# Clustered attention with a softplus network: another issue order, other engines for the movable operations, and no split of V where nothing reads it

## The chip, the cores and the metric

The kernel runs on one core of a Trainium2 chip. The metric is device time in microseconds for one execution, as the median of several runs. A core has five engines with an instruction queue each: TensorE (PE; matmuls and transposes, results in PSUM), Vector (DVE), Scalar (ACT), Pool (GpSimd) and Sync (SP), which here issues the DMAs. Each queue runs in the order in which its instructions were written; engines wait for each other through semaphores.

## The reference

Four batches, eight heads, 768 positions, head dimension 64. Every query and every key is assigned to the nearest of 16 centroids of its head (by cosine), and a query attends only to keys of its own cluster. The result, 3072 rows of 512, goes through a two-layer network with softplus. Everything is float32.

```
q_assign = argmax(q_n @ c_n^T)      # per head; k_assign in the same way
mask     = q_assign[:, None] == k_assign[None, :]
scores   = where(mask, (q @ k^T) / sqrt(64), -1e9)
attn     = softmax(scores);  x = attn @ v          # x: 3072 x 512
h        = x @ w_in                                # 512 -> 2048
out      = (max(h, 0) + log1p(exp(-abs(h)))) @ w_out   # 2048 -> 512
```

## The kernel before

Float32 values are split in two float16 parts, high (a cast) and low (the value less its high part), and a product is the sum of three float16 matmuls (four with the mask). So nearly every operand needs a cast (line 276, `cast`) and a subtraction.

The work is cut into eight passes (batch, half of the positions) of eight heads with three query tiles each: 192 tiles, numbered t. Tile t belongs to head n, pass pi.

Preparation. `prep_k(n)` loads K of a pair of heads, casts it, subtracts, turns it (on TensorE for the first two pairs, by DMA for the others) into `kT0`, multiplies it with the centroids (`sim_k`, L562), marks the nearest one, counts the keys of each cluster (L701), and turns the marked form into `kT1`. A DMA (`lift`, L538) writes one extra row. `prep_q` and, for the first four heads of the first pass, `first_q` (in two halves u of two heads) do the same for q: products (`sim_q`), marks, the minimum with the live clusters (L868), the maximum of it (L869), the multiply of q's high part by it (L879) with a small one (L886), and the turn into `qT1`. `prep_v(n)` loads V of a pair, casts it into the middle columns of `vb` (`vh`) and subtracts into the first ones (`v`, L467). `prep_weights(step)` decodes one block of the weights (Scalar L390, Vector L392 and L396, a cast, a subtraction).

Tiles. The first 36 tiles (`UPRIGHT`) go the way of `upright(t)`: a masked product m (L942), its negated row maximum on Vector (L954), a transpose of that on TensorE (`turned`, L961), a copy `u` of it into the extra row of q, the product u (L981, L982) with keys on the partitions, and the exponential on Scalar (L1025), which gives float32 weights. Their value product (`attend`, L1137) uses the float32 V tile and float32 weights. The others go through `scores(t)`: product (L1051), row maximum (L1067), exponential (L1075), cast `ph`, subtraction `p` (L1089), for each pair of tiles one DMA transpose (`pt<-phl`, L295), and a value product of 18 float16 matmuls (L1141 to L1143) with both parts of V. `ffn1` and `softplus` follow for each pass (names `gh`, `g`), then `ffn2`; the last two passes use a form with seven products instead of eight.

Order. Each of these functions is a chain (a Python generator) that yields its operations one after the other. Nothing is planned at build time: `PLAN` is a string of base-36 numbers, two characters each, and entry by entry says which chain gives its next operation. So each engine's queue is the sequence of the operations of that engine in `PLAN`. `either(key, ...)` yields an operation that two engines can do; a name in `SWAPPED` takes the second one. A name is a kind and a tile, head, step or pass: `p41` is the subtraction of tile 41, `wh7` the cast of weight step 7. `FILL` gives, for TensorE's n-th operation, how many warm-up matmuls (L257: 128x120, results never read) are put ahead of it.

Buffers are rings: a chain that takes a buffer waits in TensorE's, Vector's or another queue until the old one is free.

Of the kernel before, what the change touches and what calls it, by code (L numbers as in the profile page):

```python
# [36 lines left out]
SWAPPED = ('E1_0', 'S1l_1', 'S1l_3', 'S2_1', 'S2_3', 'S2h_0', 'S2l_0', 'S3l_0', 'S3l_2', 'S4_0', 'S4_2', 'S4_3', 'S4h_2', 'S4l_1', 'S4l_2', 'T1a_0', 'T1a_2', 'T1c_0', 'T1c_3', 'T1h_3', 'T1l_1', 'T2a_2', 'T2c_1', 'T3a_0', 'T3a_1', 'T3a_2', 'T3a_3', 'T3b_0', 'T3b_1', 'T3b_2', 'T3c_1', 'T3l_1', 'T3l_3', 'T4c_0', 'T4h_2', 'T4h_3', 'T4l_0', 'T4l_2', 'g0_3', 'g0_5', 'g1_1', 'g2_5', 'g5_7', 'g6_0', 'g6_1', 'g6_4', 'g6_5', 'g6_6', 'g7_1', 'g7_2', 'g7_4', 'g7_5', 'g7_6', 'g7_7', 'gh1_6', 'gh2_4', 'gh3_1', 'gh5_6', 'gh7_0', 'gh7_2', 'gh7_3', 'gh7_5', 'k0_0', 'k0_1', 'k14', 'k18', 'k22', 'kT0_0_0', 'kT0_2_1', 'kT1_2_0', 'kT1_2_1', 'm12_2_0', 'm12_3_0', 'm20_4_0', 'm28_7_0', 'm8_2_0', 'm8_3_0', 'p100', 'p101', 'p103', 'p136', 'p170', 'p172', 'p173', 'p175', 'p177', 'p178', 'p180', 'p181', 'p182', 'p183', 'p184', 'p185', 'p186', 'p189', 'p190', 'p191', 'p38', 'p39', 'p40', 'p42', 'p45', 'p46', 'p47', 'p59', 'p61', 'p64', 'p67', 'p71', 'p72', 'p79', 'p82', 'p85', 'p89', 'p90', 'p92', 'ph175', 'ph178', 'ph180', 'ph184', 'ph186', 'ph189', 'ph58', 'ph62', 'ph83', 'ph86', 'ph87', 'q0_0_0', 'qT1_1', 'u1', 'u11', 'u13', 'u21', 'u23', 'u27', 'u31', 'u33', 'u35', 'v8', 'vh14', 'vh18', 'w15', 'w19', 'w20', 'w23', 'w29', 'wh17', 'wh24', 'wh29', 'wh30', 'wh7', 'wh9', 'x0_2', 'x2_0', 'x6_3', 'x7_0', 'x7_1', 'x7_2', 'x7_3', 'xh0_3', 'xh1_3', 'xh2_3', 'xh3_0', 'xh3_3', 'xh6_3', 'xh7_0', 'zk10', 'zk12', 'zk16', 'zk18', 'zk2', 'zk20', 'zk4', 'zq0_1', 'zq8_2')  # L37
# [10 lines left out]
    "1xc7c6c61zc61xc8c7c7c6c721211w23231z0a21211z1y210d252023ce0bcfc9cac8cbcc21caca25252723c822c9c9c8ca2723c92325"
    "2927270d2b22220a222925cdce25242b2b29272d29260d0dcccbcccecd2d2729292fcf222b28cc0ace2f2h2f0d2d2f2d2bcb22cccgch"
    "ci2h2j2a0d0d0dcgcg2b2h2dcf0dcf0d0dcd2j2c2d2f2e0dcf0dcf0d0d22cjcd2fcbcb2h2e2e2e2l2j2j0d0d2l2n2nchci2echcgch2g"  # L50
    "2h2h2j2l2n2lcgcgck2jch2nce2p2p2i2l2k2p2l2r2ncicicjci2p2rcdchcl2ncjcj2m2p2t2r0eckckckck2t2p2rcj2e2ecicmcjce2o"
    "2r2r2v2v2t2q2t2v2t2q2q2qcl2x0e0e0e2v2tck2q2q2s2v2v2x2z2z2x2xcmclcmclcm2ucn2q312z2x312w0e0e0e0e0e0eco2z2x2zcl"
    "2z33333131cl2y310fcncn0e0e0ecncz33353531cmcmcpcq33czcncococo33dpcn35cz37370f0f0fcoczdqdqdp353037320ecocr3335"
    "37dp0e0e0e39cz0hdqdqdq3232323439czcp32cqcpcpcqcq32323539370f0f3b3936dsdsdsczcpcp37crcq3b390fcrcrcrcr393d0fcz"
    "3bcz3b0ecs3d3d3b0f0f0f3dczdtdt0h3bdudu0f0fdtdt0hcqdt383d0i3d3f3f3aczctcscsducs3f3h3f3f3c3jcz3edv3h3jcscs0gcu"
    "0i0i0i3h3ld0ctdw3hct3h3hdw3edw3j0g3ncz3edv3edwczd0ctcu3l3n0i3j3l3pdy3edyctdwd0cu0g0j0kcucu3l3n3ndy3e3eczczdz"
    "3gdz0i3p0i3i3rcuctcv3l0iczcz3j3l3p3t3p0g3ndzczdz0iczdz3rd03p3pcve0e03t3r3ve0cz3ke10jcvcv3tcz3xe1cv3te23m0id0"
# [1634 lines left out]
```

## Time and profile before

| | |
|---|---|
| time, median of three runs (lowest to highest) | 811.96 us (811.94 to 812.08) |
| span of the profiled execution | 809.7 us |
| outside of the span (median less span) | 2.3 us |
| TensorE busy | 799.3 us, 99% |
| Vector, Scalar, Pool busy | 597.8, 548.4, 473.8 us |

The profile shows one execution. The span goes from the first to the last instruction; its own time is not given, and the difference to the median is taken to be the same before and after. A busy TensorE is not TensorE at its peak, since matmuls are pipelined and each is shown some 0.16 us longer than the distance to the next. Idle time of an engine counts only where the work that ends last waits for it.

### The profile page before, as it was taken

How to read it: one execution, taken by the hardware profiler on the slowest of the kernel's cores; microseconds unless marked ns; L12 is line 12 of the kernel's file. 1: busy time of each engine (PE TensorE's matmuls, PEld its weight loads, DVE VectorE, ACT ScalarE, POOL GpSimd, SP SyncE). 2: the span in 40 equal slices, each digit the busy share in tenths (PEclk: the TensorE clock that was granted, in tenths of full speed). 3: DMA queues.
4: the chain of work that ended last, by engine and by line, in shares of the span. 5: the costliest groups of instructions: out<-in, count | busy, mean ns of one | idle time of the engine just before them, and what ended most of it. 6: DMA issues, size and time to landing. Idle time of an engine off the chain costs nothing.

```text
span 809.7 us, 19600 instructions
## 1 busy us (share of the span) xinstructions
PE 799.3 (99%) x8086; PEld 543.1 (67%) x8086; DVE 597.8 (74%) x1005; ACT 548.4 (68%) x851; POOL 473.8 (59%) x351
## 2 busy tenths in 40 slices
PE   8999999999999999999999999999999999999998
PEld 8898987655666666656666656666666656576787
DVE  7889998887976877766664547658554868887796
ACT  6777689865877777658587577677676667645441
POOL 4645456555656577745677585687578562613453
PEclk9999999999999999999999999999999999999999
DMA  9976769999999999999899989999898687730101
GB/s 257 244 185 157 218 148 225 205 219 201 173 175 181 184 207 200 216 204 174 155 162 188 189 171 186 206 209 168 171 165 177 115 145 129 128 60 1 47 1 60
DMA packets 390474, 133.71 MB, mean 165 GB/s; under 512 B 367088, under 2 KB 383984, under 8 KB 390384
## 3 DMA queue, kind: packets, MB, share of 16 engines
q1 hardware_dynamic: 390384, 132.46, 81.8%
q8 instruction: 63, 1.03, 0.5%
q14 instruction: 27, 0.22, 0.1%
HBM read 35.68 MB, written 6.29 MB: 52 GB/s over the span
## 4 chain that ended last, share of the span: by engine, by line
PE 77%; DMA 5%; DVE 2%; ACT 1%; POOL 1%; issue 0%; SPq 0%; DVEq 0%; ACTq 0%; POOLq 0%
PE s L1051 11%; PE h L1212 9%; PE h L1214 9%; PE h L1213 9%; PE o L1613 7%; PE o L1615 7%; PE o L1614 7%; DMA pt<-phl 4%; PE mbank L1141 3%; PE mbank L1143 3%; PE mbank L1142 3%; PE m L1491 2%; PE m L1492 2%; PE m L1490 2%; PE mbank L1137 1%; POOL phl L1089 1%
## 5 line engine op out<-in xcount | busy, mean ns | idle before, releaser
L1089 POOL TENSOR_TENSOR phl<-p,phl 128x768 f16<-128x768 f32 x117 | 194.1, 1667 | 123.9 <-ACT phl L276 94.5
L1067 DVE TENSOR_REDUCE negm<-s 128x1 f32<-128x768 f32 x156 | 147.9, 952 | 51.1 <-PE s L1051 49.6
L1075 ACT ACTIVATE p<-s,negm 128x768 f32<-128x768 f32 x156 | 139.5, 896 | 65.9 <-DVE negm L1067 50.8
L1212 PE MATMUL h<-xT,wi 128*128 128x384 f16 x512 | 166.8, 326 | 0.4 <-DVE fg L1249 0.4
L1214 PE MATMUL h<-xT,wi 128*128 128x384 f16 x512 | 167.0, 326 | 0.0
L1213 PE MATMUL h<-xT,wi 128*128 128x384 f16 x512 | 166.9, 326 | 0.0
L276 ACT CAST phl<-p 128x768 f16<-128x768 f32 x145 | 118.7, 829 | 21.1 <-DMA pt<-phl 19.0
L1051 PE MATMUL s<-kt,qt 128*128 128x384 f16 x624 | 126.2, 326 | 0.0
L1233 ACT ACTIVATE fa<-h 128x384 f32<-128x384 f32 x128 | 62.3, 488 | 75.8 <-PE h L1214 75.2
L1613 PE MATMUL o<-wo,gh 128*128 128x512 f16 x288 | 109.1, 379 | 0.4 <-DVE ot L1636 0.4
L1615 PE MATMUL o<-wo,gh 128*128 128x512 f16 x288 | 109.2, 379 | 0.0
L1614 PE MATMUL o<-wo,gh 128*128 128x512 f16 x288 | 109.2, 379 | 0.0
L1249 DVE SCALAR_TENSOR_TENSOR fg<-fa,h 128x384 f32<-128x384 f32 x104 | 56.8, 549 | 62.3 <-ACT fa L1234 54.8
L1141 PE MATMUL mbank<-vb,pt 128*128 128x65 f16 x936 | 99.8, 193 | 0.8 <-DMA pt<-phl 0.7
L1142 PE MATMUL mbank<-vb,pt 128*128 128x64 f16 x936 | 99.8, 192 | 0.0
L1143 PE MATMUL mbank<-vb,pt 128*128 128x65 f16 x936 | 99.6, 194 | 0.0
L1141 PEld LDWEIGHTS <-pt 128*128 128x128 f16 x936 | 86.8, 98 | 12.6 <-DMA pt<-phl 2.4
L1142 PEld LDWEIGHTS <-pt 128*128 128x128 f16 x936 | 86.2, 97 | 10.0
L1272 POOL TENSOR_TENSOR gh<-fg,gh 128x768 f16<-128x768 f32 x43 | 72.3, 1683 | 27.7 <-ACT gh L276 27.5
L1143 PEld LDWEIGHTS <-pt 128*128 128x128 f16 x936 | 86.3, 97 | 0.0
L1051 PEld LDWEIGHTS <-qt 128*128 128x128 f16 x624 | 58.3, 98 | 39.8
L1214 PEld LDWEIGHTS <-wi 128*128 128x128 f16 x512 | 49.9, 98 | 33.2
(300 smaller groups left out, 1622.7 us busy)
## 6 DMA issues: line engine op xcount, KB each, us to landing
wo<-in_moe_w_in_dram SPq DMA_DIRECT2D x16, 512.0 KB, 5.1
wo<-in_moe_w_out_dram SPq DMA_DIRECT2D x14, 512.0 KB, 4.2
rawk<-in_k_dram SPq DMA_DIRECT2D x15, 384.0 KB, 4.4
rawq<-in_q_dram SPq DMA_DIRECT2D x15, 384.0 KB, 4.4
rawv<-in_v_dram SPq DMA_DIRECT2D x12, 384.0 KB, 4.1
out_dram<-ot SPq DMA_DIRECT2D x18, 256.0 KB, 2.7
rawv<-in_v_dram SPq DMA_DIRECT2D x8, 192.0 KB, 5.4
pt<-phl SPq DMA_TRANSPOSE x78, 5.9
```

The costliest lines, as they stand in the source:

```text
L1051: nc.tensor.matmul(st[:, j, :SH], qt[:, s, i], kt[:, s, NT // 2 * j : NT // 2 * (j + 1)], start=(s == 0), stop=(s == 1),)
L1067: yield op("DVE", 950, lambda: nc.vector.tensor_reduce(negm, st[:, :, :SH], AX.XY, ALU.max, negate=True))
L1089: lambda e: e.tensor_tensor(phl[:, u, 1], p32, phl[:, u, 0], ALU.subtract),
L1141: nc.tensor.matmul(av, pt[:, 0, c], vb[:, c, D : 2 * D + 1], start=(c == 0), stop=False)
L1142: nc.tensor.matmul(av[:, :D], pt[:, 0, c], vb[:, c, :D], start=False, stop=False)
L1143: nc.tensor.matmul(av, pt[:, 1, c], vb[:, c, D : 2 * D + 1], start=False, stop=(c == NT - 1))
L1212: nc.tensor.matmul(hp, w[0], x[0], start=(c == 0), stop=False)
L1213: nc.tensor.matmul(hp, w[0], x[1], start=False, stop=False)
L1214: nc.tensor.matmul(hp, w[1], x[0], start=False, stop=(c == NP - 1))
L1613: nc.tensor.matmul(po, g[0], wo[:, f, 0, 0], start=(f == f0), stop=False)
L1614: nc.tensor.matmul(po, g[0], wo[:, f, 0, 1], start=False, stop=False)
L1615: nc.tensor.matmul(po, g[1], wo[:, f, 0, 0], start=False, stop=(f == f0 + NF // 2 - 1))
```

## The change

Four things change, and no operation of the computation is different.

- `FILL` is a new table: 88 warm-up matmuls instead of 175.
- `SWAPPED` is a new list. 227 operations change sides: 86 go from Scalar to Pool and 11 from Pool to Scalar (all casts), 74 from Pool to Vector and 29 from Vector to Pool (subtractions and a few products), 17 from Vector to Scalar and 10 from Scalar to Vector (copies and marks).
- `PLAN` is a new string. TensorE's first operation and its last 398 of 1002 stand where they stood (the last third of the run), those between are in another order. The other queues' last 86 to 355 operations also stay.
- `prep_v` leaves out the cast and the subtraction for the pairs of heads of which no tile needs split V: pairs 0 and 1 of the first batch. Two casts (`vh0`, `vh2`) and two subtractions (`v0`, `v2`) go. A small operation also gets a name of its own (`mw_0`, `mw_1`; it was `m0_0_0`, `m0_0_1` like the one ahead of it), so that it can have its own side.

```
-FILL = {0: 40, 3: 12, 4: 21, 6: 11, 10: 11, 14: 28, 16: 23, 18: 8, 19: 8, 22: 7, 25: 6}
+FILL = {0: 27, 1: 12, 2: 3, 8: 11, 9: 7, 14: 13, 15: 5, 18: 7, 24: 3}
...
+    unsplit = {n // 2 for n, _, _ in tiles} - {n // 2 for t, (n, _, _) in enumerate(tiles) if not is_whole(t)}
...
-        yield cast(f"vh{n}", 830, 1290, vb[:, :, :, D : 2 * D], vf)
-        yield either(
-            f"v{n}",
-            ("POOL", 1640),
-            ("DVE", 950),
-            lambda e: e.tensor_tensor(vb[:, :, :, :D], vf, vb[:, :, :, D : 2 * D], ALU.subtract),
-            shared=True,
-        )
         vkey[n // 2] = vk
+        if n // 2 not in unsplit:
+            yield cast(f"vh{n}", 830, 1290, vb[:, :, :, D : 2 * D], vf)
+            yield either(
+                f"v{n}",
+                ("POOL", 1640),
+                ("DVE", 950),
+                lambda e: e.tensor_tensor(vb[:, :, :, :D], vf, vb[:, :, :, D : 2 * D], ALU.subtract),
+                shared=True,
+            )
...
-            f"m0_0_{u}",
+            f"mw_{u}",
...
-SWAPPED = (...)
+SWAPPED = (...)
-PLAN = (...)
+PLAN = (...)
```

What the first entries of both strings say, queue by queue (a and b are the halves of a pair or of q; a number in brackets is the count of warm-up matmuls ahead; m0, u0, turned0 belong to tile 0):

```
TensorE before: [40] kT0_0a, centroids, kT0_0b, [12] sim k0, [21] qT0a, kT0_2a, [11] qT0b, sim qa,
   count k0, kT0_2b, [11] sim qb, sim k2, kT1_0a, kT1_0b, [28] count k2, kT1_2a, [23] qT1a, kT1_2b,
   [8] m0, [8] m1, qT1b, turned0, [7] turned1, m2, u0, [6] turned2, m3, u1, attend0, m4, turned3, u2
TensorE after:  [27] kT0_0a, [12] kT0_0b, [3] centroids, qT0a, sim k0, sim qa, kT0_2a, kT0_2b,
   [11] qT0b, [7] count k0, sim k2, kT1_0a, sim qb, kT1_0b, [13] qT1a, [5] kT1_2a, count k2,
   m0, [7] kT1_2b, turned0, m1, u0, m2, turned1, [3] m3, attend0, qT1b, turned2, turned3, m4, u1
Vector before:  centroid norm, k0a low, scaled, k0b low, scaled low, kT0_0a, kT0_0b, k0 max, qa low,
   k0 x4, k0 mark, qa x2, count k0, qa x2, qb x2, qa min, k2 x5, qb, qa max (L869), qb, count k2,
   qb min, qb max, kT1_0b, kT1_2a, weights x2, max0, max1, qT1b, max2
Vector after:   k0a low, centroid norm, scaled, scaled low, qa low, kT0_0b, k2 low, k0 max, qa max,
   k0 x2, qa, k0 x2, qa x2, count k0, qa min, k2 max, qa max (L869), k2, qb, k2 x3, qb, qT1a, qb x2,
   count k2, max0, qb min, kT1_2b, qb max, max1, weights, max2, mw_1, weights, max3
Scalar before:  norm, norm, k0a, k0b, k2, centroids, qa, qb, qT0a, kT0_2a, qT0b, kT0_2b, weights, vh0,
   kT1_0a, k2 mark, weights x2, vh2, qT1a, kT1_2b, k4, u0, k6, exp0
Scalar after:   k0a, norm, k0b, norm, qa, kT0_0a, centroids, qT0a, qb, kT0_2a, kT0_2b, k0 mark, qT0b,
   kT1_0a, kT1_0b, k2 mark, kT1_2a, u0, weights, exp0, k6, q4, u1
Pool before:    ..., k2 low, qb low, qa, qa mark, qb, qb mark, qa multiply x2, qb multiply x2, v0, k4 low
Pool after:     ..., k0b low, k2 cast, qb low, qa, qa mark, qa multiply x2, qb, qb mark, k4 cast, k4 low,
   qb multiply, k6 low
SP before:      k0a, k0b, k2, w0, qa, qb, v0a, w1, v2a, v6a, v0b, w2, lift0, v6b, v2b, v4a, w3, k4, k6
SP after:       k0a, k0b, qa, k2, qb, v0a, v0b, w0, lift0, w1, k4, k6, lift2, w2, q4, turn k4, w3
```

## Rows read from the trace of the kernel before

**Rows 1.** The page, busy time of each engine and its share of the span

```profile
PE 799.3 (99%) x8086; PEld 543.1 (67%) x8086; DVE 597.8 (74%) x1005; ACT 548.4 (68%) x851; POOL 473.8 (59%) x351
```

**Rows 2.** Windows: busy us of each engine, granted clock, DMA share, GB/s

```profile
core 0: us, PE busy (x) PEld busy (x) DVE busy (x) ACT busy (x) POOL busy (x), PEclk, DMA share, GB/s
50.00:110.00 60.00, 58.18 (x637) 52.72 (x635) 55.21 (x98) 45.14 (x79) 30.66 (x28) 1.00 0.74 191
110.00:600.00 490.00, 488.36 (x4897) 305.65 (x4896) 347.36 (x575) 357.18 (x537) 313.10 (x213) 1.00 0.98 188
806.00:809.70 3.70, 0.62 (x6) 0.30 (x4) 0.42 (x1) 0.00 (x0) 0.00 (x0) 1.00 0.22 76
```

**Rows 3.** TensorE's waits: us in total, times, longest

```profile
PE mbank L257 <- DVE ones L230: 1.5, 1, 1.5
PE m L942 <- ACT ptf L1025: 0.9, 2, 0.5
PE mbank L1141 <- DMA pt<-phl: 0.7, 2, 0.4
```

**Rows 4.** Timeline of TensorE: start, us, what [idle before, released by]

```profile
1.51 4.16 PE L257 MATMUL mbank<-ones,eye 128*128 128x120 f16 x40 [1.51 <-DVE ones L230]
...
7.52 0.17 PE L562 MATMUL sim_k<-cents,kt 128*128 128x16 f16 x1 [0.28 <-ACT cents L339]
...
11.08 0.17 PE L562 MATMUL sim_q<-cents,qt 128*128 128x16 f16 x1
...
14.04 1.63 PE L257 MATMUL mbank<-ones,eye 128*128 128x120 f16 x28
16.40 0.26 PE L701 MATMUL sim_k<-kn,ones 128*128 128x192 f16 x1 [0.72 <-ACT kn L648]
...
18.72 0.50 PE L899 MATMUL qT<-eye,qn 128*128 128x128 f16 x6 [0.44 <-DVE kt L480]
...
20.11 0.50 PE L942 MATMUL m<-kt,qt 128*128 128x384 f16 x2
...
25.85 1.50 PE L1137 MATMUL mbank<-rawv,ptf 128*128 128x65 f32 x12
```

**Rows 5.** Timeline of Vector, the start

```profile
5.58 0.34 DVE L328 SCALAR_TENSOR_TENSOR cb<-cfs,crn,cb 128x128 f16<-128x128 f32 x1
...
10.00 0.36 DVE L592 TENSOR_REDUCE best_k<-sim_k 128x12 f32<-128x192 f32 x1
10.39 0.37 DVE L594 TENSOR_TENSOR sim_k<-sim_k,best_k 128x192 f32<-128x192 f32 x1
...
15.97 0.24 DVE L869 TENSOR_REDUCE aq<-qn 128x6 f16<-128x96 f16 x1
```

**Rows 6.** Timelines of Scalar and of Pool, the start

```profile
14.28 0.83 ACT L276 CAST vb<-rawv 128x768 f16<-128x768 f32 x1 [0.81 <-DMA rawv<-in_v_dram]
...
7.17 1.64 POOL L631 TENSOR_TENSOR kn<-rawk,kn 128x768 f16<-128x768 f32 x1 [3.99 <-ACT kn L276]
...
16.88 0.83 POOL L879 TENSOR_TENSOR qn<-qn,aq 128x384 f16<-128x384 f16 x1
...
19.39 1.78 POOL L467 TENSOR_TENSOR vb<-rawv,vb 128x768 f16<-128x768 f32 x1
```

**Rows 7.** DMA issues of the first 7 us: KB each, median us from issue to landing

```profile
rawk<-in_k_dram SPq DMA_DIRECT2D x2, 192.0 KB, 2.4
...
rawq<-in_q_dram SPq DMA_DIRECT2D x2, 192.0 KB, 5.1
```

**Rows 8.** Groups by line: count, busy us, mean ns, idle before by releaser

```profile
L954 DVE TENSOR_REDUCE negu<-m 128x1 f32<-128x768 f32 x36 | 34.1, 953 | 5.3 <-PE m L942 4.9
```

**Rows 9.** Casts and subtractions by engine; the last row: ns min/median/max, first and last start

```profile
L1089 POOL TENSOR_TENSOR phl<-p,phl 128x768 f16<-128x768 f32 x117 | 194.1, 1667 | 123.9 <-ACT phl L276 94.5 <-issue 13.9 <-PE sim_k L563 5.2
L276 ACT CAST phl<-p 128x768 f16<-128x768 f32 x145 | 118.7, 829 | 21.1 <-DMA pt<-phl 19.0
...
L276 POOL CAST phl<-p 128x768 f16<-128x768 f32 x11 | 9.7, 885 | 22.3 <-ACT p L1075 13.3 <-DMA pt<-phl 8.6 <-ACT fa L1234 0.2
...
L1089 DVE TENSOR_TENSOR phl<-p,phl x39: 942/957/2392, 139.3 to 708.8; 128x768 f16<-128x768 f32 x39
```

More of the change, by code (lines that the diff above doesn't have):

```diff
@@ L48 @@
[L48 to L57, printed above, removed]
@@ new lines @@
+    "d501d4d9d4d4c3d906d401d506d4dbd506d50106da0106d406c4d4d406d506dcded4d5d5d51fdcd51fd5061f061f1h1fd51h080b1jc3"
+    "08dd1f08c51h0bc3d51jd5091l1g09c308d51h1jc41l1lc61nd5c5c41h1n081h1n1p1r1i1n080b1p1j0b1p1t1r081t1j080b1p1r1l1t"
+    "09c60a1vc3c70b1j1lc81r08c70b07081k08c51ldf1v1n09c5c91x1n091v0b1mc6c41x1z1pc6070c1o1xc30bdfc71v1p0b1zc6ca2109"
+    "0bc521c81r09091rcbdg1t091q2109c41q1z091tc81qc61q1v1xc908c909ca1zdjdh1sc4djdh1t1x1u1vdjdkdjc80a1q21c71xcbca1z"
+    "21dkc50ddl0d1z21cacc1wc8c8dk0dc92325231ycdcc2523c92725290dcb2027cd2b22cb2923252b222d1q22di270b232d0d0d0a29ce"
@@ new lines @@
+    "27dk220d23250d250d27c7cdc7dm2b0d0acf27c9242f0d2dcc0dce29cg2f2h2hcb2226cf29cf2f0c2j29cachcb0d2h280d2bcg222j0d"
+    "2l2fch2b2d2b2h2lcgcc2a2j2n2d2c2n2d2f2f2p2echcd0d0dcgcfcf2p2eca2r2ecgcd1q2j2h222h2p2n2l2l2r2j2r2r2ech2t2p2j2n"
+    "cfccch0c2g2t2vcicj2l2eci2ecg2l2tcj2i2vci2ncd2x2tci2xck2kch2nci2z2vck2pcj2p2z0e2x2mck2zcjcj31ckcc2o310ecl2x0e"
+    "332r2qcick2vcm2r332t2q2qcl35ck332q35cm0e2q312q2s2t0e2e0ecmcjcl0e0e332vcm350ecl0e2vcmcnce0e2u372z0a2x2x31cece"
+    "2q0eczcnczcnclcl2wco372z0edp39cmcz2z2ycn39ce3b31cz3b0f0c0edpcococpco30cq310f37350e0fdp39320e3dcncz3d3332codq"
@@ new lines @@
+    "codqcn0e3739cpcz3dcq0c33dqdqcr32cz3b3537cp0edscr35cz0hcp390f37cqcrds3fdtcrcr3239cqdtds343fcpdtcz0hcrcq0hcz3b"
+    "cs3h3fcq0f3bdudt36dq3fdu3h3dcs3bdu38cscsczcp0f3d0ics0f3hdtctcscu3j3dcz0f0g32czctdv0f0f3adv3j3h3fcz3h3jdvcudw"
+    "0gdw3hct0i3l3l3ldw0f3ncz3n0i3ncz0f3p3c3jdxcuczdvcuctcu0idvdx323e0g0fd0dx3pdycz3lctdydx3r3n3e0ke0cz3ecue0d03j"
+    "3e3l3e3p3ne0cz0i3r3g0icv0ie1ct3i3r0icvcv3tcz3pe13lcze13p0jcze23tcz0i0i3pdxcv3k3m0k3t0ke2e3e3e2e30g3v3vd0e30i"
+    "0kcve23x3o3qd03v3ze10i3qe5cz0j0jcz3re43te53z0me13xd0cvcz3vcw3r3e3te63xe60ie6czcwe3e73te73vd00k3q0m0g410kcw3z"
@@ L108 @@
+    "ioiod0d0d0d0czczimimioimioiqiqiqird0d0ipipipioikilikczczd0d0czisisisczczczd0iuisiud0itiuczczisivivivivczd0cz"
+    "ili4d0isiviviwiwj0ixiwixixivixizixixiod0d0d0d0d0d0d0d0d0d0d0d0isizisj0iyixivixizj0j4j1j3j3j3j2j1i1j5d0d0d0d0"
+    "d0irird0d0d0d0d0j7j7d0d0j6j1j6j6d0j2j2j8j8d0d0d0d0d0d0d0j9jaj9jbj9d0d0d0d0d0jcjdjcjejcd0d0d0d0d0d0d0jfjfd0d0"
+    "d0d0jgjg"
 )
```

103 lines of the change are left out of this document (47 added, 56 removed).

## The prediction

> **What bounds the kernel now.** I read the page first. TensorE is busy for 799.3 of the 809.7 us of the span, Vector for 597.8, Scalar for 548.4 [rows 1]. The windows say the same of every stretch after the start: TensorE is busy for 58.18 of the 60 us from 50 to 110, and for 488.4 of the 490 from 110 to 600 [rows 2]. So time can only come from three places: TensorE's gaps, work on TensorE that computes nothing, and useful work that is slower than it could be. The list of TensorE's waits is short: 1.5 us before its first instruction, then nothing over 0.9 us in total for one cause [rows 3]. The gaps come to 809.7 - 799.3 = 10.4 us, of which 1.5 lie before the start and 3.1 behind the last matmul (0.62 busy in the last 3.7 us [rows 2]); 5.8 are inside. The work that computes nothing is the warm-up matmul of line 257. There are 175, all within the first 25 us: 40 take 4.16 us at the start, later ones 0.055 us each (1.63 us for 28, the last one's tail included) [rows 4]. That is 4.0 + 135 x 0.055 = 11.4 us. They stand where TensorE would otherwise wait, so they are the visible form of a slow start: the first masked score product (L942, I call it m0) begins only at 20.11 us [rows 4]. After it, 29 warm-up matmuls and 4.4 us of gaps are left (5.8 less 0.28, 0.72 and 0.44 [rows 4]).
>
> **The change, part by part.**
>
> *Start.* The sum is the chain to m0. Before, Vector ends the centroids' scaled copy at 5.92 and the marks of K pair 0 at 10.76, but the first maximum over the kept queries (L869) starts only at 15.97, queued behind K pair 2's five steps [rows 5]. Pool multiplies at 16.88, TensorE turns at 18.72, m0 follows at 20.11 [rows 4, 6].
> In the new order q's first half is SP's fourth DMA and no longer its sixth: it leaves at 2.13 instead of 3.12, and only two 192 KB halves of K stand ahead of it instead of 768 KB of K and 512 KB of weights. Those halves took 2.4 us to land [rows 7]; I take 3 us, landing at 5.1. Bounds: 2.4, or the 5.1 us that it took before.
> Scalar now casts K's first half before the logarithm, so the centroids come later: cast to 4.11, logarithm 0.20, second cast 0.51, exponential to 5.1; six Vector steps of about 0.23 us give the scaled copy at 6.5 (before 5.92). TensorE turns it at 6.6, Scalar's copy (0.47 us) ends at 7.4. Vector turns to q's low part (6.5 to 7.0), K's second copy (to 7.5) and K pair 2's low part (0.95, to 8.4), which was on Pool for 1.64 [rows 6]. So K pair 0's products run at 7.5, as before (7.52). But q's first half is turned at 7.1, copied by 8.3, and multiplied with the centroids at 8.3; before it was 11.08.
> From 8.4 Vector alternates K pair 0 (five steps of 0.39) and q (0.27 each): K's marks end at 10.75, q's at 11.3, the K count is reduced by 11.9, q's minimum by 12.15, one 0.37 us step of K pair 2 goes between, and the maximum ends at 12.8. Pool's 0.83 + 0.23 us then end at 13.95, TensorE's six transposes at 14.35. Vector's copy (0.55) waits behind six short steps and ends at 15.55; behind K pair 2's turn and count, m0 begins at 15.7. Gain 20.1 - 15.7 = 4.4 us. Ends: 5.1 if that copy goes at once; 2.4 if q lands 2 us later than I take it.
>
> *SP's queue.* K pairs 4 and 6 and q's heads 4 to 7 are now loaded ahead of V pairs 2, 4 and 6; the fill of K's extra row, which waits for K pair 0's products (8.2 us), stands ahead of them all. Heads 0 and 1 read V pair 0 alone, whose halves go out sixth and seventh, and V pair 2 is first read six tiles later, so I cost the moves at 0; if V pair 2 came late, the seventh value product would wait, bounded by the 4 to 5 us of one load's landing [rows 7].
>
> *Warm-up matmuls.* 175 become 88. Those ahead of m0 are inside the 4.4. Behind m0, 29 become 10: 19 x 0.055 = 1.0 us, a gain if TensorE then has work. One group of six transposes (0.33 us) moves from ahead of m0 to behind it: -0.3.
>
> *Split of V.* Pairs 0 and 1 lose two casts on Scalar (0.83 us each, the first with 0.81 us of waiting for V in front) and two subtractions on Pool (1.78 us the first) [rows 6]. None feeds TensorE, since these heads use the float32 tile. The first cast stood ahead of a copy of turned K in Scalar's queue; what that is worth is inside the 4.4. Alone I cost it at 0, bounds 0 and 1.6 us (the 0.83 + 0.81).
>
> *Stretch after m0, to about 110 us.* The score products are issued earlier here, the float32 value products later. The 36 row maxima waited 4.9 us for these products [rows 8], and that is what the new order feeds. But Vector is busy for 55.2 of 60 us from 50 to 110 [rows 2], and now it is pressed at once: up to the fourth row maximum it has ten instructions (four maxima of 0.95, three steps of q 0.52 + 0.25 + 0.3, one copy 0.55, two weight steps 0.42 + 0.69), 6.5 us and 0.4 from m0's end, where TensorE has only 4.8 us to do: five groups of two matmuls or six transposes at 0.33, one score product 0.67, a value product 1.3 (1.50 with its tail), six transposes 0.33, three turns of 0.11, ten warm-ups. So at least 2.1 us of gaps remain. Before, 4.4 us were left; I take 4.4 again, between 2.1 and 8.3.
>
> *Sides of the middle, 110 to 600 us.* 86 casts go from Scalar to Pool, 11 back; 74 operations, mostly subtractions, go from Pool to Vector, 29 back. A cast of 128x768 takes 0.885 us on Pool and 0.829 on Scalar; the subtraction 1.667 on Pool and 0.957 on Vector, where nothing holds it [rows 9]. Scalar loses some 60 us, Vector gains at most 45 x 0.957 = 43 in 490 us. It was busy for 347 of these 490 us (71%) [rows 2] and comes to 80%; TensorE waited there for 490 - 488.4 = 1.6 us in all [rows 2], 0.7 of them for pt [rows 3]. I cost it at 0; the ends are -1.6 (those waits gone) and +10.5 (the slower rival below); I stay near the lower one, since it rests on rows of this very stretch. From about 600 us on the order and the sides are as before: 0.
>
> *Sum.* 4.4 + 1.0 - 0.3 + 0 = 5.1 us: the span goes from 809.7 to 804.6, and with the 2.3 us that lie between span and median, 811.96 to 806.9.
>
> **Rivals.**
> [...]
> [...]
> *Vector eats the gain.* Asked for an unbroken run, Vector may still be busy for only 55.2 of every 60 us [rows 2]. Each 11.5 us of its work then cost 1 us of gap on TensorE, and the 45 us of work that follow m0 cost 3.9: 810.8. For: it is pressed at once. Against: it waited for TensorE more than TensorE for it.
> *The start is not passed on.* The DMA share is 0.98 from 110 to 600 us [rows 2]. If the transposes of P cannot begin earlier, TensorE waits for them what it has gained: 812. Against: a full queue would show as long waits for pt, and there are two of 0.4 us [rows 3].
> *Slower.* A Vector subtraction that meets a Pool instruction is held: 957 ns in the median, 2392 at most [rows 9]. With more subtractions on Vector and more casts on Pool, held ones delay the next row maximum, that one the exponential, the split and the transpose, and the value product waits as it did twice (0.35 us each [rows 3]). From 15 such waits the gain is gone; if half of the some 60 pairs in the reordered stretch wait so, 30 x 0.35 = 10.5, and 806.9 + 10.5 = 817.4. Against: Pool loses 45 long subtractions.
> [...]
>
> **How the numbers follow.** Forecast 0.55 (806.9; its own range 803.9 to 808.9: m0 at 15.0 and 2.1 us of gaps, or m0 at 17.7), slow clock 0.13 (807.8), Vector 0.11 (810.8), not passed on 0.09 (812), slower 0.12 (817.4). A change of 0.2%, 1.6 us, is about what a measurement of this kernel tells from none. Faster: 0.55 + 0.13 + half of 0.11 = 0.73; same 0.15; slower 0.12. The range, 803.8 to 812.0, leaves out the slower case and what lies past either end of the forecast's own.
>
> **What would show it.** Right: m0 near 15.7 us, 88 warm-ups, q's first half landing near 5, TensorE busy for about 794 us, gaps after m0 of 3 to 5 us, the last third of the span shifted as a whole. Wrong: m0 after 18 us; warm-ups at 0.10 us beyond 5.6 us (slow clock); gaps at turned between 20 and 100 us (Vector); gaps at the value products from 130 us on, waiting for pt (not passed on, or, with Vector subtractions near 2 us ahead of them, the slower case).

## The result, and the profile after

The changed kernel takes 821.32 us (median; 819.0 to 827.4), the one before 811.95. The ratio is 1.0126, 95% interval 1.0089 to 1.0164: 9.4 us slower where 5.1 us faster had been forecast. The profiled execution has a span of 818.6 us, 14.0 more than the 804.6 of the sum. Of its four executions two ran at a mean granted clock of 1.000 and took 819.0 and 820.4 us, the others 822.3 us at 0.998 and 827.4 at 0.992; so 7 to 8.5 us of the loss are there at the full clock.

The page and the windows answer to [rows 1, 2]; columns as there. The last fence of the three is the kernel before, in a window that was not shown: 84 to 500 us.

```profile
PE 798.5 (98%) x7999; PEld 538.4 (66%) x7999; DVE 633.9 (77%) x1043; ACT 491.5 (60%) x781; POOL 476.3 (58%) x379
```

```profile
50.00:110.00 60.00, 56.85 (x600) 51.26 (x599) 52.98 (x89) 40.37 (x73) 32.90 (x33) 1.00 0.72 194
84.00:500.00 416.00, 407.44 (x4101) 261.18 (x4099) 331.57 (x531) 246.10 (x389) 259.25 (x203) 1.00 0.96 184
110.00:600.00 490.00, 483.48 (x4844) 301.27 (x4843) 375.04 (x606) 303.14 (x466) 313.80 (x235) 1.00 0.99 187
```

```profile
84.00:500.00 416.00, 413.85 (x4168) 266.77 (x4166) 304.38 (x502) 303.81 (x464) 258.31 (x180) 1.00 0.96 190
```

TensorE now idles 3.2 us between 50 and 110 us (before 1.8) and 6.5 us between 110 and 600 (before 1.6). From m0 to 110 us it idles 7.5 us; before it was 2.6. From 84 to 500 us Vector went from 304 to 332 us of work, Scalar from 304 to 246, Pool stayed.

TensorE's waits (us in all, times, longest), against [rows 3], where nothing after the start was over 0.9 us:

```profile
PE mbank L1143 <- DMA pt<-phl: 2.3, 5, 1.0
PE turned L963 <- DVE negu L956: 1.8, 2, 1.6
PE turned L963 <- DVE qt L971: 1.5, 1, 1.5
PE mbank L257 <- DVE ones L230: 1.5, 1, 1.5
PE sim_q L562 <- DVE fg L1251: 1.4, 1, 1.4
PE u L983 <- ACT ptf L1027: 1.4, 2, 0.9
PE u L983 <- DVE negu L956: 1.3, 2, 0.9
PE h L1214 <- DVE fg L1251: 1.1, 1, 1.1
```

No single cause, but several waits of 1 us and more, released by Vector for the most part. The timeline of the changed kernel shows what stands behind two of them (start, us, engine, line, operation; in brackets the idle time before and who ended it; below, a wait that is counted as lost time is some 0.16 us longer than its idle time, since that much of it is shown as busy):

```profile
15.96 0.49 PE L944 MATMUL m<-kt,qt 128*128 128x384 f16 x2
...
20.85 2.17 DVE L396 SCALAR_TENSOR_TENSOR wo<-wo,wi 128x512 int32<-128x512 int32 x1
22.95 0.94 DVE L956 TENSOR_REDUCE negu<-m 128x1 f32<-128x768 f32 x1
...
20.84 1.64 POOL L633 TENSOR_TENSOR kn<-rawk,kn 128x768 f16<-128x768 f32 x1 [0.41 <-ACT kn L276]
...
23.95 0.32 PE L963 MATMUL turned<-eye,negu 128*65 128x128 f32 x1 [1.64 <-DVE negu L956]
...
176.77 1.15 POOL L404 TENSOR_TENSOR wo<-wraw,wo 128x512 f16<-128x512 f32 x1
...
177.94 0.83 ACT L276 CAST phl<-p 128x768 f16<-128x768 f32 x1 [1.35 <-POOL wo L404]
178.68 0.52 ACT L1236 ACTIVATE fa<-fa 128x384 f32<-128x384 f32 x1
...
179.23 0.55 DVE L1251 SCALAR_TENSOR_TENSOR fg<-fa,h 128x384 f32<-128x384 f32 x1 [2.59 <-ACT fa L1236]
...
179.84 0.33 PE L562 MATMUL sim_q<-cents,qt 128*128 128x32 f16 x7 [1.41 <-DVE fg L1251]
```

m0 begins at 15.96 us [rows 4: 20.11], 0.26 from the forecast. Then: at 20.85 a weight step of Vector takes 2.17 us (it takes 0.69 undisturbed) beside a subtraction of Pool whose recorded start is 0.02 us earlier; the row maximum of tile 3 is queued behind it, and TensorE waits 1.64 us. At 177.94 Scalar's cast waits for Pool, the softplus logarithm is queued behind the cast, Vector's step behind the logarithm, and TensorE waits 1.41 us.

The first of the two is an accident of this execution. Six later runs have the same queues up to there (e8, e10, e14 twice, e15, e16), and in each of their profiles Pool's recorded start is 0.02 us ahead as well, but Vector's step takes 0.68 to 0.69 us, Pool's subtraction 2.21, and TensorE does not wait. One of them (e14, 10 warm-ups):

```profile
20.90 0.68 DVE L396 SCALAR_TENSOR_TENSOR wo<-wo,wi 128x512 int32<-128x512 int32 x1
...
20.89 2.21 POOL L633 TENSOR_TENSOR kn<-rawk,kn 128x768 f16<-128x768 f32 x1 [0.41 <-ACT kn L276]
```

What those six, e3 and the changed kernel share between 28 and 77 us are five waits of the same length: idle 0.36, 0.88, 0.85, 0.52 and 0.49 us, together 3.1. The second of them comes from a queue place, without any hold: on Scalar the exponential stands behind the logarithm of a weight step.

```profile
30.24 0.67 ACT L390 ACTIVATE wi<-wo 128x512 f32<-128x512 f32 x1
30.93 0.81 ACT L1027 ACTIVATE ptf<-u 128x768 f32<-128x768 f32 x1
...
31.79 0.22 PE L983 MATMUL u<-qt,kt 128*128 128x128 f16 x1 [0.88 <-ACT ptf L1027]
```

To place the loss I compared each start of a TensorE operation with the shortest time of the work queued ahead of it (each operation at the lower quartile of its kind in the kernel before; the start of the span counts as lost). Lost microseconds up to TensorE's n-th operation; the times are those of the kernel before:

```
operation      30    75   120   180   260   340   500   980
at, us         28    54    85   125   194   261   392   792
before       16.5  17.6  20.5  21.5  22.2  23.2  23.4  24.6
after        14.0  17.7  19.8  23.5  27.1  29.7  32.2  33.4
```

The lead of 4.15 us at m0 is gone at 54 us; behind the 500th operation both lose 1.2 us, so the last third was shifted as a whole. From 85 us on the new order loses 13.6 us and the old one 4.1: 9.5 us, nearly the whole difference.

### The profile page after: what moved, and what is told of

Its sections match the earlier page's. It is cut to its first block, busy times and chain, and to the rows that moved or that the text cites. A ratio compares the mean times of both kernels' runs of the same rounds, so it can differ in the third digit from the quotient of the medians.

```text
span 818.6 us, 19408 instructions
## 1 busy us (share of the span) xinstructions
PE 798.5 (98%) x7999; PEld 538.4 (66%) x7999; DVE 633.9 (77%) x1043; ACT 491.5 (60%) x781; POOL 476.3 (58%) x379
## 4 chain that ended last, share of the span: by engine, by line
PE 64%; DMA 10%; POOL 6%; DVE 5%; issue 2%; ACT 2%; POOLq 0%; DVEq 0%; ACTq 0%
PE s L1053 9%; DMA pt<-phl 9%; PE h L1214 7%; PE h L1215 7%; PE h L1216 7%; PE o L1615 6%; PE o L1616 6%; PE o L1617 6%; POOL phl L1091 3%; PE mbank L1143 3%; PE mbank L1145 2%; PE mbank L1144 2%; PE m L1492 2%; PE m L1494 2%; PE m L1493 2%
## 5 line engine op out<-in xcount | busy, mean ns | idle before, releaser
L1091 POOL TENSOR_TENSOR phl<-p,phl 128x768 f16<-128x768 f32 x99 | 169.2, 1714 | 90.3 <-ACT phl L276 64.4
L1143 PE MATMUL mbank<-vb,pt 128*128 128x65 f16 x936 | 98.4, 193 | 2.4 <-DMA pt<-phl 2.3
L1145 PE MATMUL mbank<-vb,pt 128*128 128x65 f16 x936 | 98.2, 194 | 0.0
L276 ACT CAST phl<-p 128x768 f16<-128x768 f32 x103 | 84.5, 828 | 15.3 <-DMA pt<-phl 12.0
L276 POOL CAST phl<-p 128x768 f16<-128x768 f32 x53 | 46.4, 881 | 71.6 <-DMA pt<-phl 34.9
L1091 DVE TENSOR_TENSOR phl<-p,phl 128x768 f16<-128x768 f32 x57 | 65.4, 1152 | 9.8 <-ACT phl L276 4.2
```

The costliest lines, as they stand in the source:

```text
L1091: lambda e: e.tensor_tensor(phl[:, u, 1], p32, phl[:, u, 0], ALU.subtract),
L1143: nc.tensor.matmul(av, pt[:, 0, c], vb[:, c, D : 2 * D + 1], start=(c == 0), stop=False)
L1145: nc.tensor.matmul(av, pt[:, 1, c], vb[:, c, D : 2 * D + 1], start=False, stop=(c == NT - 1))
```

## The experiments

Times are medians (lowest to highest), ratios are to the kernel before on the same chip. All are built from orders, sides and warm-ups of the two kernels. "Unsplit" is the kernel before with only the split of V left out.

**1. The split of V alone.**

```
+        if n // 2 not in unsplit:    # order, sides, FILL of before
```

> The kernel before with nothing changed but the split of V for pairs 0 and 1, which is left out (same order, same sides, same 175 warm-up matmuls). Theory: these four instructions fed nothing that TensorE waits for, and the warm-ups stand in the queue in any case, so m0 stays at 20.1 us and the time at 812 us, within 0.5. Rival: the casts that waited for V in Scalar's queue held up the start, then m0 comes up to 1 us earlier and the time is 811 us or less.

812.04 us (811.6 to 813.0), ratio 0.9999 (0.9990 to 1.0008). The split is worth nothing that shows beside 0.7 us of noise.

**2. The new start alone, the new order alone, the new sides alone.**

```
e2:  PLAN, SWAPPED: of after for what began before 20.4 us in it, then of before;  FILL of after
e3:  PLAN of after;   SWAPPED of after up to 84 us, then of before
e4:  PLAN of before;  SWAPPED of before up to 84 us, then of after
```

> The changed kernel's order, sides and warm-ups for all that it began before 20.4 us, and from there the order and the sides of the kernel before. Theory: the 4.2 us by which m0 came earlier are real, and it is the later order and sides that gave them back with more: 808 us (806.5 to 809.5). Rival: whatever follows, Vector and the DMAs cannot take the earlier start on, so the gain is gone by 110 us: 812 us or more.

818.04 us (815.8 to 823.1), ratio 1.0078 (1.0051 to 1.0105). m0 begins at 15.91 us, yet the end is later than in the kernel before. The rival's number holds: the lead is lost without the later order, though on a seam that neither kernel has. The lead goes within eight microseconds of m0, at a copy that waits for two weight steps, which Pool holds (1.74 us for both; 0.42 each undisturbed):

```profile
20.64 1.64 POOL L633 TENSOR_TENSOR kn<-rawk,kn 128x768 f16<-128x768 f32 x1
...
21.16 1.74 DVE L392 TENSOR_SCALAR wi<-wi 128x512 int32<-128x512 int32 x2 [0.49 <-ACT wi L390]
22.93 0.29 DVE L971 TENSOR_SCALAR qt<-turned 1x128 f16<-1x128 f32 x1
...
23.27 0.32 PE L963 MATMUL turned<-eye,negu 128*65 128x128 f32 x1 [2.89 <-DVE qt L971]
```

Then the granted clock is 0.50 from 24.4 to 27.9 us, and a value product that takes 1.50 us takes 2.16: that is part of the 6 us (the executions ran at mean clocks of 0.990 to 0.998). From 29 us on its TensorE queue is that of before, and most waits of before come back to 0.01 us, except for new ones of 1.4 us at 258 and 2.1 us at 283. Those two led to experiments 3 and 4.

> The changed kernel's order throughout and its sides up to 84 us; after that every movable operation has its engine of before. If the new sides of the middle make the loss (Vector held by Pool, Vector subtractions that wait for casts on Pool), the 9 us lost from 84 to 340 us come back: 812 us. If the order makes it, 819 to 821 us as before.

> The counterpart: the order of the kernel before throughout (without the split of V), its sides up to 84 us, and after that the sides of the changed kernel (194 operations). If the sides make the loss: 820 us. If the order makes it: 812 to 813 us. If only both together do: below 815 us here and in the counterpart.

865.49 us (863.4 to 866.1) and 875.10 us (871.8 to 875.8), ratios 1.065 and 1.077. I had given both theories times under 822; both missed. The new order with the old sides is 44 us slower than with its own, the old order with the new sides 63. In both profiles the granted clock was 0.50 for some 20 us, by my estimate some 10 us of that. So what is "the order's" and what "the sides'" can't be told apart by swapping.

**3. The old order, moved by a microsecond or two.**

```
 FILL = before's
e5:   +45: 25       e13:  +45: 10  and  +45: 50
e6:   -18: 8, 19: 8, 22: 7, 25: 6
```

> The kernel before with unsplit V left out (812.0 us), and 25 more warm-up matmuls, 25 x 0.055 = 1.4 us, in front of TensorE's 46th operation (35.5 us). No order, side or wait differs. Theory 'any shift costs' (the order before fits only its own times: moved by a microsecond, Vector's and Pool's instructions meet that did not meet before, as at 257 and 282 us of the run with the new start): new waits of TensorE appear between 60 and 340 us, and the time is 815 us or more. Rival 'a shift is just a shift': the schedule behind 35 us moves as a whole, 812.0 + 1.4 = 813.4 us, or less where a later wait takes it up.

815.05 us (814.6 to 815.4), ratio 1.0036 (1.0023 to 1.0049): a delay of 1.4 us costs 3.0. The queues are the same instruction by instruction, and the timelines say what differs. First unsplit, then the delayed kernel, at the same place:

```profile
275.33 1.56 ACT L276 CAST phl<-p 128x768 f16<-128x768 f32 x2 [1.02 <-DMA pt<-phl]
...
275.76 0.24 DVE L836 TENSOR_SCALAR n<-eq_q 128x192 f16<-128x192 f16 x1
276.03 0.36 DVE L916 TENSOR_TENSOR eq_q<-eq_q,al 128x192 f16<-128x192 f16 x1
276.30 2.00 DVE L1069 TENSOR_REDUCE negm<-s 128x1 f32<-128x768 f32 x2
...
276.24 3.26 POOL L1091 TENSOR_TENSOR phl<-p,phl 128x768 f16<-128x768 f32 x2 [2.19 <-ACT phl L276]
```

```profile
276.79 1.56 ACT L276 CAST phl<-p 128x768 f16<-128x768 f32 x2 [0.50 <-DMA pt<-phl]
...
277.70 3.25 POOL L1091 TENSOR_TENSOR phl<-p,phl 128x768 f16<-128x768 f32 x2 [1.42 <-ACT phl L276]
...
277.74 1.71 DVE L836 TENSOR_SCALAR n<-eq_q 128x192 f16<-128x192 f16 x1
279.48 1.68 DVE L916 TENSOR_TENSOR eq_q<-eq_q,al 128x192 f16<-128x192 f16 x1
281.08 0.94 DVE L1069 TENSOR_REDUCE negm<-s 128x1 f32<-128x768 f32 x1
...
283.07 0.81 PE L1053 MATMUL s<-kt,qt 128*128 128x384 f16 x4 [1.47 <-ACT p L1077]
```

In the delayed kernel Scalar's casts, which wait for a transfer to free their buffer, come 0.52 us sooner against the work around them. So Pool's subtractions begin 0.04 us ahead of Vector's small step, where they began 0.48 us behind it. The small steps, 0.24 and 0.36 us, become 1.71 and 1.68; the row maximum behind them is 2.8 us late, and TensorE waits 1.47. Something that came sooner made the kernel slower. The same happens at 418 us, and TensorE loses 0.98 us at 423.

> The kernel before with unsplit V left out (812.0 us) and 10 more warm-ups, 0.55 us, in front of TensorE's 46th operation. Theory 'the moments decide': either no new wait (812.6 us) or new ones of 1 to 2 us each at places where a step of Vector and a subtraction of Pool start within half a microsecond of each other (813.5 to 816 us). Rival 'a shift is just a shift, and what cost 3 us with 25 warm-ups was something else': 812.6 us within 0.4.

> The same with 50 more warm-ups, 2.75 us. In step with its delay it would come to 814.8 us; in proportion to the run with 25 (3.05 us for 1.4) to 818.0. Theory 'the moments decide': out of step with both, since other pairs meet, between 814.8 and 819 us. Rival 'shift': 814.8 us within 0.4.

812.48 us (811.3 to 814.4), ratio 1.0005 (0.9996 to 1.0014), and 819.50 us (815.4 to 821.5), ratio 1.0085 (1.0061 to 1.0108). In both profiles the start is 1.2 us late besides (q's first halves land in 6.2 us; in the run with 25 it is 0.5 late). With 0.55 us the whole is taken up but for 0.3 in the profile: two waits of 0.5 and 0.7 us, at 467 and 425 us, shrink to 0 and 0.3. Both theories allowed that. At the place shown above its Vector is 0.66 us ahead of Pool, and nothing is held:

```profile
276.91 1.56 ACT L276 CAST phl<-p 128x768 f16<-128x768 f32 x2 [1.19 <-DMA pt<-phl]
...
277.16 0.24 DVE L836 TENSOR_SCALAR n<-eq_q 128x192 f16<-128x192 f16 x1
...
277.82 3.25 POOL L1091 TENSOR_TENSOR phl<-p,phl 128x768 f16<-128x768 f32 x2 [1.81 <-ACT phl L276]
```

The casts come within 0.12 us of those of the run with 25, Vector 0.58 us sooner. With 2.75 us the median moves by 7.5: new waits of 1.6 us at 259 and 2.2 us at 424, behind the same steps (L596, L836, L916), held for 1.6 to 1.8 us each. Out of step with the delay, as the moments theory said, and 0.5 us above its range.

> The kernel before with unsplit V left out (812.0 us), and without the 29 warm-up matmuls behind the first masked product (1.6 us). The term of the prediction (0.055 us each, a gain if TensorE then has work) gives 812.0 - 1.6 = 810.4 us. Rival 'TensorE waits there anyway': the place of the warm-ups is taken by gaps for the row maxima and the time stays at 812.0 within 0.5 us. Theory 'any shift costs': 813 us or more, with new waits between 60 and 340 us.

816.36 us (815.9 to 819.2), ratio 1.0060 (1.0042 to 1.0078). In its profile q's first halves take 6.6 us to land [rows 7: 5.1] and the whole start is 1.5 us late, so it is not a clean test. But up to the 45th operation it stays 1.5 us late: new gaps between 21 and 26 us take the place of the 1.6 us of warm-ups. The term did not appear. The wait that the kernel with unsplit V ends at 57.8 us ends at 59.3 to 59.6 in the profiles with 10 and 25 warm-ups and in this one, and behind 85 us they lose 2.9, 5.6 and 6.9 us: the size of the shift alone does not say what it costs.

**4. Two row maxima moved ahead of the held steps.** On top of the 25 warm-ups:

```
 Vector:  -zq12_3, keep q12_3, max 78, max 79      -zq16_5, keep q16_5, max 114
          +max 78, zq12_3, max 79, keep q12_3      +max 114, zq16_5, keep q16_5
```

> The delayed kernel (25 more warm-ups at 35.5 us; 815.05 us) with two moves in Vector's queue and nothing else: zq12_3 (L836) and the multiply behind it (L916) stand behind the row maxima of tiles 78 and 79 and no longer ahead of them, zq16_5 and its multiply behind the row maximum of tile 114. Those were the four instructions that waited up to 1.7 us each for Pool's subtractions p76, p77, p112 and p113; the row maxima read PSUM and were 0.95 us in every row, beside Pool or not. Theory 'Vector held by Pool, with row maxima queued behind': TensorE's waits of 1.63 us at 281 us and 0.98 us at 421 us go, 815.05 - 2.6 = 812.4 us, at most 813.5. Rival 'the held steps are only a symptom, the waits come from late transfers or from the delay itself': the two waits stay or come back within a few tiles, 814.5 us or more.

```profile
277.76 0.95 DVE L1069 TENSOR_REDUCE negm<-s 128x1 f32<-128x768 f32 x1
278.62 1.23 DVE L836 TENSOR_SCALAR n<-eq_q 128x192 f16<-128x192 f16 x1
279.75 0.94 DVE L1069 TENSOR_REDUCE negm<-s 128x1 f32<-128x768 f32 x1
280.61 0.96 DVE L916 TENSOR_TENSOR eq_q<-eq_q,al 128x192 f16<-128x192 f16 x1
...
278.11 3.24 POOL L1091 TENSOR_TENSOR phl<-p,phl 128x768 f16<-128x768 f32 x2 [1.98 <-ACT phl L276]
```

In the profiled execution the maxima pass beside Pool at 0.95 us, the small steps are still held, the wait of TensorE at 283 us is gone and the one at 423 falls from 0.98 us to 0.59; the span is 811.4 us against 813.0, of which 0.5 is a start that is 0.5 us earlier. But the median is 814.47 us (813.2 to 816.3), ratio 1.0033 (1.0020 to 1.0045), against 1.0036: over all executions nothing is shown to be won. That the maxima inherit the hold is shown at this place; the time is not bought back, and the theory's 813.5 is missed.

**5. Repairs in the new order.**

```
e7:   Vector: step0#3, step1#2 behind max 5;  Scalar: step3#1 behind exp 2;  u30 Vector -> Scalar
e11:  e7, and  Scalar: softplus 0/15#1 ahead of ph46;  Vector: softplus 1/9#2 ahead of p65
e10:  L1091 on Pool:  -tensor_tensor(128x768)   +2 x tensor_tensor(128x384)
```

> The changed kernel (819 to 822 us in most of its runs) with four moves: Vector's weight steps 0 (third part, L396) and 1 (L392) stand behind the row maximum of tile 5 and no longer ahead of those of tiles 3 and 4; Scalar's logarithm of weight step 3 stands behind the exponential of tile 2; the copy u30 is on Scalar again. Theory 'useful steps queued ahead of the row maxima and copies cost the lead': the gaps of 1.8 us at tile 3's turn (22 us), 1.0 at u3 (30 us) and 1.7 at tile 31's turn (94 us) go, the lead over the kernel before at 54 us is 2 to 3 us instead of none, and the time falls by 3 to 4.5 us, to about 816. Rival 'Vector has no room there' (it is busy all the time): the gaps come back at the next row maxima, the lead at 54 us stays under 1 us, and the time stays at 819 to 822.

817.39 us (815.3 to 821.1), ratio 1.0070 (1.0043 to 1.0098). The waits at 22 and 94 us go, the one at 31 us falls to a third (a new one of 1 us comes at 27); at the 75th operation 16.0 us are lost, 1.6 less than in the kernel before, where 2 to 3 had been expected. Some 4 us of the 9.4 come back by the medians; the two intervals touch (the changed kernel's begins at 1.0089), but e11, built on this one, is clear of it. What brings them back is for the larger part the copy u30: TensorE idles 1.5 us for it in all six profiles that leave it on Vector behind the new order's weight steps (changed, e10, e14 twice, e15, e16), and in four of the six the granted clock then falls to 0.50 for 3.4 us or more; here both are gone. The moves of the weight steps are not shown to help: by the comparison above this kernel is some 1 us ahead at 85 us, and e3, e8, e15 and e16, which lack the moves, are 0.6 to 1.7 ahead.

> The kernel with four early moves (817.4 us) and two swaps more: Scalar's logarithm of softplus step 15 of the first pass stands ahead of the cast ph46, and Vector's last step of softplus step 9 of the second ahead of the subtraction p65. Theory 'each wait of the middle is one instruction queued behind one that is late': the waits of 1.5 us at 175 us (TensorE waits for that softplus step) and 1.3 us at 244 us go, and the time is 817.4 - 2.8 = 814.6 us. Rival 'given back': the value products of tile 46 and of later tiles wait longer for their transposes, or new holds appear, and the time stays within 816.5 to 819.

817.39 us again (814.6 to 819.7), ratio 1.0065 (1.0048 to 1.0081). The two waits are gone from the profile, and waits for the transposes pt took their place: 3.9 us in six, where e7 has 1.8 us in three. Given back, as the rival said.

> The changed kernel (819 to 822 us in most of its runs) with each of Pool's 99 subtractions p (L1091, 128x768, 1.65 us) issued as two of 128x384, so that one instruction of Pool can hold Vector for about 0.9 us and no longer for 1.65. Pool's work grows by some 0.15 us each. Theory 'the length of the holds is what is lost in the middle': Vector's held instructions shrink, and the time falls by 2 to 5 us, to 816 to 818. Rival 'late casts and queue places, not the length of the holds': the same waits of TensorE, between 100 and 340 us, stay; 819.5 to 823.

824.07 us (822.9 to 827.1), ratio 1.0153 (1.0137 to 1.0169). The halves take 972 ns each, 1.94 us for what took 1.71, and the waits for pt grow to 3.5 us. It is not a clean test: Pool has 19 us more to do (its subtractions 187.9 us against 169.2), and in the profile the granted clock was 0.50 for 10.2 us (30.6 to 37.5 and 98.9 to 102.3 us). Behind those, from 125 us on, it loses 0.7 us more than the changed kernel, while Vector's held time falls from 39 to 35 us. So shorter holds are not shown to help.

**6. The new start with the old rest.**

```
e8:   e2 with the seam at 84 us instead of 20
e12:  e7 up to 80 us, then before; v4, v6, weight step 11 left where after has them
```

> The changed kernel's order, sides and warm-ups for all operations that began before 84 us in it, then the order and the sides of before. At 84 us the changed kernel is 0.5 us ahead of the one before. Theory 'the new order and sides of the middle, 84 to 340 us, cost the 9.4 us': without them the rest goes as before, 812.0 - 0.5 = 811.5 us, at most 813. Rival 'any shift costs': the old middle, reached in other times, loses too: 815 us or more, with held Vector instructions ahead of its waits.

> The start of the kernel with four early moves up to 80 us (there it is 4.3 us ahead of the kernel before), then the order and the sides of before, with the loads' followers that the new order does later (v4, v6, weight step 11) left where the new order has them, so that nothing piles up at the seam. Theory 'the lead is kept where no new hold appears': 812 - 4 = 808 us with no new hold, 1.5 us more for each, at most two of them: 808 to 811, faster than before. Rival 'any shift costs more than it brings': 812 us or more.

823.68 us (820.5 to 828.1), ratio 1.0161 (1.0131 to 1.0191), and 833.82 us (829.1 to 836.1), ratio 1.026. Both theories of a kept lead fall. In e8 the subtractions of V pile up behind the seam and hold Vector's weight steps (2.05 and 2.08 us; 0.69 undisturbed); TensorE waits 1.52 us for an exponential queued behind them, and then its clock falls (windows; columns as in [rows 2]):

```profile
83.84 3.59 POOL L470 TENSOR_TENSOR vb<-rawv,vb 128x768 f16<-128x768 f32 x2 [0.56 <-ACT vb L276]
...
83.93 2.05 DVE L396 SCALAR_TENSOR_TENSOR wo<-wo,wi 128x512 int32<-128x512 int32 x1
85.90 2.08 DVE L396 SCALAR_TENSOR_TENSOR wo<-wo 128x512 int32<-128x512 int32 x1
...
87.42 2.82 PE L1139 MATMUL mbank<-rawv,ptf 128*128 128x65 f32 x12 [1.52 <-ACT ptf L1027]
```

```profile
76.00:87.10 11.10, 9.88 (x104) 9.29 (x103) 10.86 (x11) 7.79 (x13) 9.13 (x7) 1.00 0.77 207
87.10:97.40 10.30, 9.02 (x52) 8.13 (x53) 6.91 (x13) 3.87 (x7) 6.38 (x7) 0.50 0.40 83
97.40:110.00 12.60, 10.49 (x120) 9.03 (x119) 6.54 (x14) 6.46 (x11) 1.16 (x1) 1.00 0.46 154
```

So e8 is no clean test of the old middle: by my estimate about half of the 9.0 busy microseconds in that window are the clock. From 125 us on, behind the fall, its old middle loses 0.8 us more than that of the kernel before; the changed kernel loses 6.8 more there. Nor is e12 one: already at 52 us Scalar waits 3.12 us for a load of q and TensorE 3.29 behind it, and the granted clock is 0.50 in four stretches, 17 us in all. And its price was wrong: by the comparison above e7 is 1 to 2 us ahead at 80 us, not 4.3.

**7. The new order, moved; and one part of its sides undone.**

```
 FILL = after's      e14:  +45: 10  and  +45: 40
e15:  ph of 46 tiles on their old engine (44 Pool -> Scalar)
e16:  p of 50 tiles on their old engine (34 Vector -> Pool, 16 Pool -> Vector)
```

> The changed kernel (819 to 822 us in most of its runs) and 10 more warm-ups, 0.55 us, in front of TensorE's 46th operation (34 us). Theory 'the new order itself is at fault': its waits at 178, 187, 230 and 247 us come back by name, each as long as before, and the time is 821.3 + 0.55 = 821.9 us, within 1. Theory 'the moments decide': another set of waits, and a time anywhere between 814 and 826 us.

> The same with 40 more warm-ups, 2.2 us. Theory 'the new order itself is at fault': the same waits by name, 821.3 + 2.2 = 823.5 us within 1, or less where a wait has room to take the delay up. Theory 'the moments decide': another set of waits, not in step with the delay, between 816 and 828 us.

824.41 us (822.2 to 824.7), ratio 1.0145, and 823.39 us (821.9 to 824.2), ratio 1.0136. Up to 110 us all three profiles of this order have the same waits (1.7 at u30, 1.0 twice, 0.7 twice), only the one at 22 us is missing in the moved ones. From 150 us on the sets differ: the waits at 178 and 187 us are in neither, those at 230 and 247 in one of them; new are, among others, 2.2 and 1.7 us at 286 for pt, 1.3 and 1.2 at 354, in one 1.1 at 453. So the waits do not come back by name, though the second time lies where the theory 'new order' had it. The sum does not scatter as widely as the moments theory said (one profile each; e8 and e12 are left out for their seams, and the 17.4 contain 3.4 us at a clock of 0.50):

```
lost from the 120th operation to the 980th, us
old order:  before 4.1, unsplit 4.2, +10 2.9, e9 4.3, +25 5.6, e6 6.9, +50 7.0, e2 7.1
new order:  e11 10.6, e7 11.1, after 13.6, +40 16.0, +10 17.4
```

In these profiles the level goes with the order and its sides, the single wait with the moment.

> The changed kernel (821.3 us) with only the casts ph of the score tiles on their old engines (46 of them, 44 back from Pool to Scalar), the order unchanged. Theory 'casts on Pool, with the subtraction waiting for them on Vector, carry the loss': Pool has 44 x 0.82 = 36 us less to do and Vector's subtractions find their casts done; most of the some 10 us lost in the middle go, 812 to 817 us. Rival 'the order is made for its sides': Scalar's queue has these casts at places that were chosen without them, exponentials and logarithms come later, 823 us or more.

> The changed kernel with only the subtractions p on their old engines (50 of them, 34 back from Vector to Pool, 16 from Pool to Vector), the order unchanged. Theory 'more subtractions on Vector carry the loss' (the slower case of the prediction): 812 to 818 us. Rival 'the order is made for its sides': Pool, with 18 subtractions more of 1.65 us, delays the transposes, 825 us or more.

833.23 us (830.6 to 836.9), ratio 1.026, and 843.85 us (839.6 to 845.1), ratio 1.037. Undoing either part makes it worse, as both rivals said (in e16's profile the granted clock was 0.50 for 14 us, in e15's for 3.4). Which part carries the level stays open.

## Why the prediction was wrong

*Start to m0: the number is right, the chain only in part.* Forecast 15.7 us, measured 15.96. 88 warm-ups ran, and the split of V cost nothing, also by itself. But q's first half took 4.2 us to land and not 3, at 6.3 us and not 5.1; its turn, its product with the centroids and the maximum came 0.5, 0.7 and 0.7 us late. This was absorbed where Vector's copy waits behind short steps: it ended at 15.76, forecast 15.55. That the miss fell on a queue with room was luck.

*The slow clock* (0.13, 807.8): warm-ups did go at 0.10 us beyond 5.6 us. The 12 that begin at 5.39 us went at 0.10 us each up to 6.13 and at 0.05 behind it, 1.15 us in all, after 0.41 us of idle that ended at 4.77; in the kernel before, the pace changed at 5.56, and 12 in a row took 0.79. No run shows the 0.9 us by which 807.8 lies above the forecast; m0 came 0.26 us late, and what share of that is the clock no run shows.

*The warm-ups: this term, 1.0 us, did not appear.* Its count was wrong too: eight of the 29 stand ahead of m0 (the order of TensorE before shows them as [8] m0), so 21 become 10. And experiment 3 (e6) shows gaps in the place of those that were left out.

*The stretch after m0: this step failed.* I counted at least 2.1 us of gaps and took "4.4 again", the figure of the old order for everything behind m0; up to 110 us it had only 2.6 of them. The new order has 7.5, inside my bounds of 2.1 and 8.3. Between m0 and 85 us the lead shrank from 4.15 us, plus the 1.0 for the warm-ups that were to be a gain, to 0.7. Five waits that eight profiles of this start share, 3.1 us together, are the larger part: the new order queues weight steps and copies ahead of exponentials and row maxima, and I took such waits to be no more than before without following one. The bound on Vector's ten instructions was also made with their undisturbed durations; one of them, the weight step of 0.69, took 2.17 in the profile of the changed kernel. I had priced held steps in the slower rival ([rows 9]: 957 ns in the median, 2392 at most) and not in this step. But the hold is in one of seven profiles, and the six without it are at most 1 us further ahead at 85 us.

*The sides of the middle "cost at 0": this step failed by 9.5 us* (counted from 85 us on; 6.8 of them from 125), *and it decides the sign.* In idle time, 6.5 us from 110 to 600 where there were 1.6. Its estimate of the loads was fair: I gave Vector at most 43 us more in 490, and it got 28 (347.36 in [rows 2] to 375.04, held time included). The error was to take TensorE's 1.6 us of waits in 490 us as a sign of slack. It was a property of one order at its own moments: the same queues, moved by 0.55, 1.4 and 2.75 us, lose 0.4, 3.0 and 7.5. And TensorE's busy time, another sign, was 798.5 us and not 794, because the first 0.16 us of each wait is shown as busy. A small sum of waits says that this order meets its times, not that another one would.

*The slower rival* (0.12, 817.4) had the mechanism, a Vector step held by Pool with a step behind it on which TensorE waits, and it shows at 20.85 us (2.17 us for 0.69) and in all four kernels that move the old order and lose (e2, e5, e6, +50). Its price was wrong in kind: not thirty waits of 0.35 us but, from 84 to 500 us, fifteen lost stretches over 0.25 us, up to 1.7, and by several chains: a cast behind Pool's weight step, a copy behind weight steps, a transpose late for the value product.

*What stays open.* Why the new order loses 10.6 to 17.4 us behind its 120th operation and the old one 2.9 to 7.1, in one profile each. Vector busier by 27 us in 416 (332 against 304) fits, since it has less room to take up a late step, but no run varied that alone. Vector's held time from 84 to 500 us (durations over the shortest of their kind in the same profile) tells the orders apart badly: 33 us in the old order, 31 with 10 warm-ups, 38 in its other moved kernels, 39 to 44 in the new one. Pool's held time tells them apart at once: 9.5 to 11 us in every profile of the old order, 26 to 28 in the changed kernel and those of e7, e11 and e14. With more subtractions on Vector, Pool is often the one that has to wait, and a cast or subtraction that Pool ends late makes a transpose late. That fits the waits for pt, but no run varied it alone; shorter holds are not shown to help, and undoing casts or subtractions broke the order. That the old order had been fitted to times measured on the chip would explain why most moves hurt it; no run shows it.

## What to carry to other kernels

A schedule without waits is not a schedule with slack: before costing a reordering at nothing, move the old one by several amounts around a microsecond and see what that costs. Steps that Pool held (here 1.71 us for 0.24) belong behind the steps on which TensorE waits, not ahead of them, and a count of an engine's work has to price such steps at their held duration; here this removed a wait in the profile, but no time. An order and its engine sides are one thing: halves of the change told nothing about it here. Before the time of a rebuilt kernel is read as the price of an order, its granted clock has to be read too.
